# Where 64-bit weights are loaded and converted: w_out's chunks spread over pass 1, w_in's moved into pass 1

## The chip, the cores and the metric

The kernel runs on one core of one Trainium2 chip. The metric is the time of one execution on the device in microseconds (us); runs are summarised by their median.

## What is computed

The reference chains three stages. The first is the real part of a two-dimensional Fourier transform of `x` (8 batches of 3072 rows and 256 columns):

```
X = np.fft.fft(x, axis=1)
X = np.fft.fft(X, axis=2)
return X.real.astype(np.float32)
```

Its 24576 rows then pass through a soft mixture of experts (8 experts with 4 slots each), and last through a layer with a squared ReLU:

```
logits = x @ phi
d = softmax of logits over all rows;  slot_input = d.T @ x
slot_out[e] = np.maximum(slot_input[e] @ w1[e], 0.0) @ w2[e]
c = softmax of logits over slots;     x = c @ slot_out
h = x @ w_in;  r = np.maximum(h, 0.0);  g = s * (r * r) + b
return g @ w_out
```

The weights `w_in` (256 x 2048) and `w_out` (2048 x 256) come as 64-bit floats. There is no 64-bit arithmetic on the chip's engines here, so the kernel loads them as pairs of 32-bit words and puts 32-bit floats together from them.

## The kernel before

The work runs in stages, and x is read twice from memory.

**Pass 1.** x comes in 24 pages of 1 MB (`load_x`, L282), three for each of the 8 batches, numbered here x0 to x23 in the order of loading. Each batch is worked on in two halves n = 2b and 2b + 1, so n runs from 0 to 15. The even half needs the batch's first two pages, the odd half its third. In `emit_v` (L383) TensorE multiplies x with the projected transform matrix into `vt`; ScalarE copies that out (L392); in `turn_v` (L401) TensorE transposes it into `vq`, and either ScalarE or VectorE copies that into `v` (L405), whichever a planner in the code believes to be free. When all four batches of a half are in `v`, `emit_t` (L420) transforms along the rows, one unit of four matmuls into `tps` at a time. There are 16 units. Each is copied into `tt` by eight small copies (L432), all eight on ScalarE for an even unit and on VectorE for an odd one. Eight units are done between n = 8 and n = 15, the other eight after the last half of x. The next stage, the logits (`lp`, L523), reads all of `tt`.

**The logits and pass 2.** After the logits and their maximum, pages of x are loaded a second time in another layout (`load_xr`, `xrt`, L316), again 24, and summed with the softmax weights into `racc` (L679). Then come the experts: `e_up` reads eight pages `w1t` (L851), `e_turn` transposes, and `e_down` reads eight pages `w2t` (L879). The last and longest stage is the layer with w_in and w_out over 64 blocks of rows (L996 to L1035).

**Pages.** Almost all of these tiles come out of one ring of 15 pages, with 5 more from the end of pass 1 on. A transfer into a page waits for the last reader of what stood there. All large transfers are issued by SyncE in the order in which the code asks for them, so one that waits for its page holds up those behind it.

**The 64-bit weights.** Each of the two matrices comes in four chunks of 1 MB (`raw`, issued at L148). For each chunk VectorE runs `double_steps`: shift, two combinations, a mask and a multiplication (L152, L156, L160, L164, L172), then a maximum (L198 for w_out, L216 for w_in). A chunk's raw page is given back after L172. For w_out, GpSimd also adds up the rows for the bias (L267). After w_out's fourth chunk the scale follows: a maximum over the four (L229), a transposition on TensorE (`mx`, L233), two small steps, and then the split of the scaled weights into two 16-bit parts (L259 on VectorE, L261 on ScalarE, L262 on GpSimd). The same three small steps for w_in's maximum (`wim_steps`) come as soon as all of w_in is converted, and at the latest inside `e_down`.

**What sets the order.** In pass 1 the string `ORDER` (L289) gives the order of the transfers: `x` a page of x, `w` a chunk of w_out, `l` and `h` the tables `ltab` and `htab_t`. `pump_a` issues them as far as pages and a lead in estimated time allow. In pass 2 and after, the list `todo` (L762 on) is worked through as pages come free. `side_step` and `fill` put the conversions' steps between the other instructions by estimated times; once built, each engine's order is fixed, and an instruction that waits holds up all that stand behind it on its engine.

Of the kernel before, what the change touches and what calls it, by code (L numbers as in the profile page):

```python
# [32 lines left out]
def tile_fft2__then__softmoe__then__act_relu2(  # L33
# [60 lines left out]
    def page(shape, dt, name, among=9):  # L94
        k = next(k for k, p in enumerate(pools[:among]) if p[2] < p[1])
        pools[k][2] += 1
        return pools[k][0].tile(shape, dt, tag="page", name=name), k

    def free_pages(among=9):
        return sum(max(p[1] - p[2], 0) for p in pools[:among])  # L100
# [4 lines left out]
    todo = []  # L105
    side_work = []
    at = {"pe": 5.0, "act": 0.0, "dve": 0.0, "dma": 3.8}

    def dma_ready(cost=2.93):

        at["dma"] = max(at["dma"], at["pe"] - 1.0) + cost
        return at["dma"] + 1.3
# [10 lines left out]
    side_at, raws, doubles = {}, [0], []  # L123
# [18 lines left out]
    def double_steps(d, src, pool):  # L142

        w = 1024
        raw, rk = page([P, w, 2], U32, "raw")
        raws[0] += 1
        hi, lo = raw[:, :, 1], raw[:, :, 0]
        nc.sync.dma_start(out=raw.rearrange("p w t -> p (w t)"), in_=src.bitcast(U32))  # L148
        f = d.bitcast(U32)

        def s1():
            nc.vector.tensor_scalar(out=f, in0=hi, scalar1=3, scalar2=0x3FFFFFF8,  # L152
                                    op0=ALU.logical_shift_left, op1=ALU.bitwise_and)

        def s2():
            nc.vector.scalar_tensor_tensor(out=f, in0=hi, scalar=0xC0000000, in1=f,  # L156
                                           op0=ALU.bitwise_and, op1=ALU.bitwise_or)

        def s3():
            nc.vector.scalar_tensor_tensor(out=f, in0=lo, scalar=29, in1=f,  # L160
                                           op0=ALU.logical_shift_right, op1=ALU.bitwise_or)

        def s4():
            nc.vector.tensor_scalar(out=hi, in0=hi, scalar1=0x7FF00000, scalar2=None, op0=ALU.bitwise_and)  # L164
            if pool:
                nc.gpsimd.tensor_scalar(out=hi.bitcast(F32), in0=hi, scalar1=float(0x38100000), scalar2=None, op0=ALU.is_ge)
                nc.gpsimd.tensor_tensor(out=d, in0=d, in1=hi.bitcast(F32), op=ALU.mult)
                done()

        def s5():  # L170
            if not pool:
                nc.vector.scalar_tensor_tensor(out=d, in0=hi, scalar=float(0x38100000), in1=d, op0=ALU.is_ge, op1=ALU.mult)  # L172
                done()

        def done():
            drop(rk)
            raws[0] -= 1

        return [(0.0, s1, 0.65), (0.0, s2, 1.15), (0.0, s3, 1.15), (0.0, s4, 0.65), (0.0, s5, 0.0 if pool else 1.15)]
# [28 lines left out]
    def wi_load(k):  # L208
        if k % 2 == 0:
            t, kk = page([P, FF2], F32, "wi", 2)  # L210
            wi.append(t)
            wik.append(kk)
        c, h = divmod(k, 2)
        d = wi[c][:, 1024 * h:1024 * h + 1024]
        steps = double_steps(d, w_in[c * P:(c + 1) * P, 1024 * h:1024 * h + 1024], False)
        steps.append((0.0, lambda: nc.vector.tensor_reduce(  # L216
            out=wim4[:, k:k + 1], in_=d, axis=AX.X, op=ALU.max, apply_absolute_value=True), 1.15))
        side_at[4 + k] = dma_ready()
        side_work.extend((4 + k, *f) for f in steps)
# [59 lines left out]
    def load_x():  # L279
        n = len(xa)  # L280
        t, k = page([P, 2, 8, P], F32, "xb")
        nc.sync.dma_start(out=t, in_=xt[3 * (n // 3) + (0, 2, 1)[n % 3]])  # L282
        xa.append((t, k))
        x_at.append(dma_ready())
# [1 line left out]
    NX = 3 * B  # L286
    CR = 1.5
    LEAD, TOL, LT, LX, HX = 14.0, 0.5, 0, 0, 1
    ORDER = "xxwxwxwxwxxxxxxxxxxxxxxxllhh"  # L289
    tpool = tc.alloc_tile_pool(name="tpool", bufs=1)  # L290
    doubles += [((3, 1, 3, 1)[k], lambda k=k: wo_load(k)) for k in range(4)]

    order = list(ORDER)

    def order_step():
        k = order.pop(0)
        if k == "w":
            doubles.pop(0)[1]()
        elif k == "l":
            ltab_load(len(ltabs))  # L300
        elif k == "h":
            htab_load(len(htabs))
        else:
            load_x()

    def pump_a():

        while order and at["dma"] < at["pe"] + LEAD and free_pages() >= (doubles[0][0] if order[0] == "w" else 1):
            order_step()

    x_at, pend_t, xr = [], [], []
# [24 lines left out]
    def htab_load(i):  # L336

        t, k = page([R, 16, 2, 4 * MH], F32, "htab_t")
        htabs.append((t, k))
        nc.gpsimd.memset(t[32:64], 0.0)  # L340
        for q in range(2):
            nc.sync.dma_start(out=t[64 * q:64 * q + M], in_=htab[:, 32 * i:32 * i + 32].rearrange("r (k q) m -> r k q m", q=2))
        dma_ready(2.5)
# [5 lines left out]
    def ltab_load(i):  # L349
        t, k = page([P, 32, P // 2], F32, "ltab")  # L350
        ltabs.append((t, k))
        for c in range(2):
            nc.sync.dma_start(out=t[NR * c:NR * c + NR], in_=ltab[64 * c:64 * c + M, 32 * i:32 * i + 32].rearrange(
                "(j g) q m -> g j q m", j=2)[0:NR // 2])
        dma_ready(1.2)

    with tc.tile_pool(name="xtp", bufs=1, side="right") as xtp, tc.tile_pool(name="vp", bufs=1, side="right") as vp, \
# [94 lines left out]
        for n in range(NV + 1):  # L452
            if n < NV:
                emit_v(n)
                pump_a()
                fill()
            if n == 3:
                tp = psv.tile([P, P], F32, tag="tps", name="tp", bufs=4)
                nc.tensor.transpose(tp, f_sb, ident)
                nc.vector.tensor_copy(ft_sb, tp)  # L460
            if n >= 1:
                turn_v(n - 1)
            for _ in range(4):
                if pend_t and n < NV:
                    emit_t()
            fill()
            pump_a()
        while order:
            order_step()
# [279 lines left out]
    def w1_load(e):  # L749
        t, wk[0, e] = page([P, 2, FF1], F32, "w1t")  # L750
        nc.sync.dma_start(out=t, in_=w1[e].rearrange("(c p) f -> p c f", p=P))
        w1t[e] = t
        dma_ready()

    def w2_load(e, h=2):
        if h in (0, 2):
            w2t[e], wk[1, e] = page([P, FF1 // P, D], F32, "w2t")
        c = (slice(0, 4), slice(4, 6), slice(0, 8), slice(6, 8))[h]
        dma_ready(2.93 * (0.5, 0.25, 1, 0.25)[h])
        nc.sync.dma_start(out=w2t[e][:, c], in_=w2[e].rearrange("(c p) d -> p c d", p=P)[:, c])  # L760

    todo += [(0, lambda: nc.sync.dma_start(out=dd, in_=dft_d.rearrange("j (c p) d -> p j c d", p=P)))]  # L762
    left = NS1 - len(xr) - sum(t[1] is load_xr for t in todo)
    todo += [(1, load_xr)] * (left - 6)
    for k in range(4):
        todo += [(2 - k % 2, lambda k=k: wi_load(k), 1 - k % 2), (1, load_xr)]
    todo += [(1, load_xr)] * 2
    todo += [(1, lambda e=e: w1_load(e)) for e in range(8)] + [(1, lambda e=e: w2_load(e)) for e in range(4)]
    todo += [(h == 0, lambda e=e, h=h: w2_load(e, h)) for h in (0, 1, 3) for e in range(4, 8)]
    pump()  # L770
# [168 lines left out]
    with tc.tile_pool(name="fr", bufs=4) as frp, tc.tile_pool(name="fo", bufs=3) as fo, \  # L939
# [104 lines left out]
        at = [k * 48 // (16 - 3) for k in range(16 - 3)]  # L1044
# [118 lines left out]
```

## Time and profile before

| | us |
|---|---|
| median of 3 runs | 1433.32 |
| lowest and highest run | 1432.83, 1433.5 |
| the profiled execution, its own time | 1434.0 |
| its span in the trace | 1432.2 |
| TensorE busy in the span | 1384.2 |
| VectorE busy | 1176.8 |
| ScalarE busy | 946.3 |
| GpSimd busy | 323.2 |

The span runs from the first to the last instruction that the profiler recorded, and the rest of the execution's own time lies around it. TensorE is busy for 97% of the span, but its share differs by stage, and a busy TensorE here also counts matmuls that run slowly. What a change in one stage is worth has to be read in that stage.

### The profile page before, as it was taken

Reading aid. Unit: us, or ns where it says so; the run is one execution under the profiler, and the core shown is the slowest. Engines: PE = TensorE matmul, PEld = TensorE weight load, DVE = VectorE, ACT = ScalarE, POOL = GpSimd, SP = SyncE. Lnnn points to the kernel's source line nnn. Section 1 sums busy time; section 2 is a strip of 40 time slices with the busy share of each in tenths; the row PEclk is TensorE's granted clock in tenths of the full one; section 3 lists DMA queues with packets and bytes.
Section 4 is the critical chain, followed back from the end, with each engine's and each line's share of the span. In section 5 each row is a group of like instructions: output and inputs, shape, how many; then the busy total and the mean of one; then the engine's idle time right before and its main releaser. Section 6 shows DMA issues by size and latency. Waiting matters only on the chain.

```text
span 1432.2 us, 23062 instructions
## 1 busy us (share of the span) xinstructions
PE 1384.2 (97%) x8930; PEld 841.2 (59%) x8930; DVE 1176.8 (82%) x1536; ACT 946.3 (66%) x1411; POOL 323.2 (23%) x298
## 2 busy tenths in 40 slices
PE   6796998899999999999999999999999999999998
PEld 4476654556666666666666666666666666666665
DVE  2767753798989898998989888888888888888885
ACT  1255510677777777777777777777777777777773
POOL 1521600431212121222222222121212121111110
PEclk9898999999999999999999999999999999999999
DMA  8995599010101010101010101010101010101000
GB/s 344 416 289 223 210 401 343 16 40 23 36 23 32 23 36 23 35 23 36 23 35 23 36 23 32 23 36 23 36 23 36 22 36 23 36 23 33 23 23 27
DMA packets 81198, 113.41 MB, mean 79 GB/s; under 512 B 35808, under 2 KB 69984, under 8 KB 74304
## 3 DMA queue, kind: packets, MB, share of 16 engines
q1 hardware_dynamic: 80960, 111.83, 23.0%
q8 instruction: 70, 1.15, 0.3%
q14 instruction: 40, 0.33, 0.1%
q0 software_dynamic: 128, 0.10, 0.0%
HBM read 79.00 MB, written 25.17 MB: 73 GB/s over the span
## 4 chain that ended last, share of the span: by engine, by line
PE 89%; DVE 5%; DMA 3%; ACT 1%; SPq 1%; issue 1%; POOL 0%; POOLq 0%; ACTq 0%
PE op L1023 45%; PE op L1025 23%; PE fhp L996 11%; PE racc L679 3%; PE vt L383 2%; DMA raw<-in_moe_w_out_dram 1%; DMA w2t<-in_moe_w_dram 1%; DVE tt L432 1%; PE dps L664 1%; DVE r L1001 1%; PE tps L420 1%; PE lp L523 1%; PE ehp L851 0%; POOL dt L584 0%; PE hp L604 0%
## 5 line engine op out<-in xcount | busy, mean ns | idle before, releaser
L1023 PE MATMUL op<-whl,rhl 128*128 128x512 f16 x3072 | 1025.9, 379 | 0.0
L1025 PE MATMUL op<-whl,rhl 128*128 128x256 f16 x3072 | 837.4, 273 | 0.3 <-DVE rhl L987 0.3
L1000 ACT ACTIVATE r<-fhp 128x768 f32<-128x768 f32 x512 | 413.1, 808 | 192.7 <-PE fhp L996 189.9
L1001 DVE SCALAR_TENSOR_TENSOR r<-fhp,r 128x768 f32<-128x768 f32 x512 | 483.9, 949 | 24.4 <-ACT r L1000 22.8
L1023 PEld LDWEIGHTS <-rhl 128*128 128x128 f16 x3072 | 300.5, 98 | 335.1
L987 DVE TENSOR_TENSOR rhl<-r,rhl 128x768 f16<-128x768 f32 x500 | 489.6, 981 | 3.2 <-ACT rhl L986 0.9
L986 ACT CAST rhl<-r 128x768 f16<-128x768 f32 x508 | 420.1, 827 | 78.1 <-DVE r L1001 77.7
L1033 POOL TENSOR_TENSOR o<-o,bias 128x256 f32<-128x256 f32 x186 | 198.3, 1066 | 886.2 <-ACT o L1032 886.2
L1025 PEld LDWEIGHTS <-rhl 128*128 128x128 f16 x3072 | 300.6, 98 | 62.7 <-DVE rhl L987 0.7
L996 PE MATMUL fhp<-ct,g 128*128 128x384 f16 x1024 | 249.9, 326 | 3.7 <-DVE r L1001 2.9
L1035 DVE SCALAR_TENSOR_TENSOR ot<-op,small,o 128x256 f32<-128x256 f32 x192 | 92.7, 483 | 105.0 <-POOL o L1033 104.8
L996 PEld LDWEIGHTS <-g 128*128 128x128 f16 x1024 | 100.1, 98 | 71.2 <-issue 3.5
L1032 ACT ACTIVATE o<-op,small 128x256 f32<-128x256 f32 x186 | 88.2, 474 | 23.3 <-PE op L1025 22.6
L383 PE MATMUL vt<-xb,phd 128*64 128x512 f32 (+3 forms) x288 | 54.7, 512 | 14.8 <-DMA xb<-in_x_turned_dram 14.8
L392 ACT COPY vts<-vt 128x512 f32<-128x512 f32 (+1 forms) x16 | 8.5, 532 | 60.5 <-PE vt L383 60.4
L383 PEld LDWEIGHTS vt<-xb,phd 128*64 128x64 f32 x288 | 26.5, 149 | 37.2 <-issue 23.5
L679 PE MATMUL racc<-xrt,dh 128*64 128x256 f32 x384 | 44.3, 382 | 0.0
L679 PEld LDWEIGHTS racc<-xrt,dh 128*64 128x64 f32 x384 | 26.4, 137 | 21.0 <-issue 6.0
L987 POOL TENSOR_TENSOR rhl<-r,rhl 128x768 f16<-128x768 f32 x12 | 20.2, 1701 | 60.0 <-DMA g<-gs 53.7
L405 DVE COPY v<-vq 128x512 f32<-128x512 f32 (+1 forms) x11 | 6.6, 598 | 32.2 <-PE vq L401 32.2
L432 DVE COPY tt<-tps 32x256 f32<-32x256 f32 x64 | 26.9, 420 | 1.6 <-PE tps L420 0.8
L432 ACT COPY tt<-tps 32x256 f32<-32x256 f32 x64 | 23.2, 363 | 6.3 <-PE tps L420 5.6
(212 smaller groups left out, 547.3 us busy)
## 6 DMA issues: line engine op xcount, KB each, us to landing
xb<-in_x_turned_dram SPq DMA_DIRECT2D x24, 1024.0 KB, 19.5
xrt<-in_x_pages_dram SPq DMA_DIRECT2D x24, 1024.0 KB, 8.3
out_dram<-ot SPq DMA_DIRECT2D x128, 128.0 KB, 1.7
w1t<-in_moe_w_dram SPq DMA_DIRECT2D x8, 1024.0 KB, 9.7
out_dram<-ot SPq DMA_DIRECT2D x128, 64.0 KB, 2.0
raw<-in_moe_w_out_dram SPq DMA_DIRECT2D x4, 1024.0 KB, 18.2
raw<-in_moe_w_in_dram SPq DMA_DIRECT2D x4, 1024.0 KB, 7.3
w2t<-in_moe_w_dram SPq DMA_DIRECT2D x4, 1024.0 KB, 11.7
```

What stands on the lines that cost most here:

```text
L383: nc.tensor.matmul(vt[64 * h:64 * h + 64, o:o + k, :], lhsT=phd[:, c, sg, :], rhs=turned(pg, c, i, k, rev), start=(c == 0 and m < 2), stop ...
L679: nc.tensor.matmul(raccs[acc][64 * h:64 * h + 64, :], lhsT=dh[:, m, g].rearrange("p j e -> p (j e)"), rhs=xr[k][0][:, g, t, :], start=(sum ...
L986: (nc.vector.tensor_copy if n < 2 and p % 4 == 2 else nc.scalar.copy)(a, r2)
L987: (nc.gpsimd if far else nc.vector).tensor_tensor(out=l, in0=r2, in1=a, op=ALU.subtract)
L996: nc.tensor.matmul(hp[:, k, :].rearrange("p (s b m) -> p s b m", s=2, b=B), lhsT=g16[:, f * P:(f + 1) * P], rhs=c, start=True, stop=True)
L1000: nc.scalar.activation(out=r, in_=hp, func=AF.Relu, scale=1.0 / (CS * CS))
L1001: nc.vector.scalar_tensor_tensor(out=r2, in0=hp, scalar=0.0, in1=r, op0=ALU.max, op1=ALU.mult)
L1023: nc.tensor.matmul(op.rearrange("p h d -> p (h d)"), lhsT=a, rhs=w.rearrange("p h d -> p (h d)"), start=(f == 0), stop=False)
L1025: nc.tensor.matmul(op[:, 0, :], lhsT=l, rhs=w[:, 0, :], start=False, stop=(f == NFC - 1))
L1032: nc.scalar.activation(out=o1, in_=op[:, 1, :], func=AF.Copy, scale=qv)
L1033: nc.gpsimd.tensor_tensor(out=o1, in0=o1, in1=bias, op=ALU.add)
L1035: nc.vector.scalar_tensor_tensor(out=ot, in0=op[:, 0, :], scalar=qv, in1=o1, op0=ALU.mult, op1=ALU.add)
```

## The change

`ORDER` is rewritten: one chunk of w_out now follows the first five pages of x, and then one each three pages; a new letter `W` stands for a chunk of w_in, and four of them stand between pages x15 and x20. The loads of w_in leave the list of pass 2, which now has the second reading of x alone. The steps of the conversion themselves are unchanged. That w_in's two converted pages are now taken in pass 1 leaves two pages fewer for other loads from there on.

```
     LEAD, TOL, LT, LX, HX = 14.0, 0.5, 0, 0, 1
-    ORDER = "xxwxwxwxwxxxxxxxxxxxxxxxllhh"
+    ORDER = "xwxxxwxxxwxxxwxxWxWxxWxWxxxxllhh"
...
+    wi_at = [0]
 
     def order_step():
         k = order.pop(0)
         if k == "w":
             doubles.pop(0)[1]()
+        elif k == "W":
+            wi_load(wi_at[0])
+            wi_at[0] += 1
...
-        while order and at["dma"] < at["pe"] + LEAD and free_pages() >= (doubles[0][0] if order[0] == "w" else 1):
+        while order and at["dma"] < at["pe"] + LEAD and free_pages() >= (doubles[0][0] if order[0] == "w" else 2 - wi_at[0] % 2 if order[0] == "W" else 1):
...
     left = NS1 - len(xr) - sum(t[1] is load_xr for t in todo)
-    todo += [(1, load_xr)] * (left - 6)
-    for k in range(4):
-        todo += [(2 - k % 2, lambda k=k: wi_load(k), 1 - k % 2), (1, load_xr)]
-    todo += [(1, load_xr)] * 2
+    todo += [(1, load_xr)] * left
```

The changed file is longer, so its lines between here and the end of pass 1 are named 5 higher than those of the kernel before. Three places show what moves.

**SyncE's queue in pass 1.** The kernel before issues its transfers in this order, after the three small constants:

```order
L282 DMA xb<-in_x_turned_dram 128x2048 x6
L148 DMA raw<-in_moe_w_out_dram 128x4x512
L282 DMA xb<-in_x_turned_dram 128x2048
L148 DMA raw<-in_moe_w_out_dram 128x4x512
L282 DMA xb<-in_x_turned_dram 128x2048
L148 DMA raw<-in_moe_w_out_dram 128x4x512
L282 DMA xb<-in_x_turned_dram 128x2048
L148 DMA raw<-in_moe_w_out_dram 128x4x512
L282 DMA xb<-in_x_turned_dram 128x2048 x15
L353 DMA ltab<-in_ltab_dram 32x1x2048 x4
```

In the changed kernel, from page x11 on (the first three chunks of w_out stand behind x4, x7 and x10):

```order
L282 DMA xb<-in_x_turned_dram 128x2048 x3
L148 DMA raw<-in_moe_w_out_dram 128x4x512
L282 DMA xb<-in_x_turned_dram 128x2048 x2
L148 DMA raw<-in_moe_w_in_dram 128x2048
L282 DMA xb<-in_x_turned_dram 128x2048
L148 DMA raw<-in_moe_w_in_dram 128x2048
L282 DMA xb<-in_x_turned_dram 128x2048 x2
L148 DMA raw<-in_moe_w_in_dram 128x2048
L282 DMA xb<-in_x_turned_dram 128x2048
L148 DMA raw<-in_moe_w_in_dram 128x2048
L282 DMA xb<-in_x_turned_dram 128x2048 x4
L358 DMA ltab<-in_ltab_dram 32x1x2048 x4
```

w_out's last chunk moved from behind x8 to behind x13, and four more transfers stand ahead of the last pages of x.

**VectorE's queue from w_out's scale to the end of pass 1.** Before (after the scale's small steps; the rows with x40 are one unit and the four of the end):

```order
L259 TENSOR_SCALAR wo<-wo,small 128x512 x8
L405 COPY v_111<-vq 128x32x16
L273 TENSOR_SCALAR bias<-bp,sb_in 128x256
L405 COPY v_111<-vq 128x32x10
L405 COPY v_112<-vq 128x32x16
L432 COPY tt<-tps 32x64x4 x8
...
L405 COPY v_112<-vq 128x32x10
L405 COPY v_112<-vq 128x32x16
L432 COPY tt<-tps 32x64x4 x40
```

In the changed kernel the split stands behind a first unit of copies into `tt` and the scale; `wi` is w_in. Behind the rows shown follow the second and third chunk of w_in with one more unit between their steps, then the fourth chunk and `L437 COPY tt<-tps 32x64x4 x40`:

```order
L437 COPY tt<-tps 32x64x4 x8
L229 TENSOR_REDUCE small<-small 128x1
L234 TENSOR_REDUCE small<-mx 1x1
...
L259 TENSOR_SCALAR wo<-wo,small 128x512 x8
L273 TENSOR_SCALAR bias<-bp,sb_in 128x256
L410 COPY v_112<-vq 128x32x10
L152 TENSOR_SCALAR wi<-raw 128x1024
L156 SCALAR_TENSOR_TENSOR wi<-raw,wi 128x1024
L160 SCALAR_TENSOR_TENSOR wi<-raw,wi 128x1024
L164 TENSOR_SCALAR raw<-raw 128x1024
L172 SCALAR_TENSOR_TENSOR wi<-raw,wi 128x1024
L410 COPY v_112<-vq 128x32x16
L437 COPY tt<-tps 32x64x4 x8
```

All 24 steps of w_in moved from pass 2 to here, and seven of the nine copies of `vq` that stood here moved to ScalarE's queue. On TensorE the transposition `mx` (L233) moved from behind the matmuls of n = 6 to behind those of n = 10.

**SyncE's queue at w2's pages**, with what each transfer waits for (`DMAHW` is an earlier transfer on the same lane, the other names the engine whose last reader must be done). Before:

```order
L760 DMA w2t<-in_moe_w_dram 128x8x256 [waits DMAHW4_49,PE_49]
L760 DMA w2t<-in_moe_w_dram 128x8x256 [waits DMAHW5_49,DVE_49]
L760 DMA w2t<-in_moe_w_dram 128x8x256 [waits DMAHW6_49,PE_49]
L760 DMA w2t<-in_moe_w_dram 128x8x256 [waits DMAHW7_49,PE_49]
L760 DMA w2t<-in_moe_w_dram 128x4x256 [waits DMAHW0_49,PE_49]
L760 DMA w2t<-in_moe_w_dram 128x4x256 [waits DMAHW1_49,PE_49]
L760 DMA w2t<-in_moe_w_dram 128x4x256 [waits DMAHW2_49]
L760 DMA w2t<-in_moe_w_dram 128x4x256 [waits DMAHW3_49,DVE_49]
```

After:

```order
L765 DMA w2t<-in_moe_w_dram 128x8x256 [waits DMAHW4_49,PE_49]
L765 DMA w2t<-in_moe_w_dram 128x8x256 [waits DMAHW5_49,PE_49]
L765 DMA w2t<-in_moe_w_dram 128x8x256 [waits DMAHW6_49,PE_49]
L765 DMA w2t<-in_moe_w_dram 128x8x256 [waits DMAHW7_49,PE_49]
L765 DMA w2t<-in_moe_w_dram 128x4x256 [waits DMAHW0_49,PE_49]
```

The waits for VectorE's conversions are gone. The page of the fourth w2 transfer used to be one that `e_up` reads (`w1t`); it is now one that the last sum of pass 2 (`racc`) reads.

## Rows read from the trace of the kernel before

**Rows 1.** Windows: length, busy of PE, PEld, DVE, ACT, POOL; PEclk, DMA share, GB/s.

```profile
13.00:57.00 44.00, 29.90 (x144) 14.53 (x144) 29.03 (x28) 5.29 (x10) 12.20 (x14) 0.88 1.02 412
57.00:99.00 42.00, 41.01 (x268) 26.19 (x269) 21.58 (x46) 20.95 (x50) 20.76 (x18) 0.96 1.01 328
...
154.00:218.00 64.00, 63.25 (x528) 36.50 (x528) 40.96 (x63) 13.81 (x26) 17.48 (x17) 1.00 0.89 346
...
232.00:251.00 19.00, 13.96 (x133) 5.72 (x131) 3.04 (x9) 0.07 (x1) 0.00 (x0) 0.82 1.12 305
```

**Rows 2.** Chain that ended last, end of pass 1: start us, us, what.

```profile
116.70 5.44 PE lp L523 x73
```

**Rows 3.** Timeline of TensorE, pass 1: start us, us, instructions, [idle before].

```profile
13.18 1.98 PE L383 MATMUL vt<-xb,phd 128*64 128x512 f32 x4 [4.55 <-DMA xb<-in_x_turned_dram]
...
49.76 3.29 PE L383 MATMUL vt<-xb,phd 128*64 128x384 f32 x12 [0.42 <-DMA xb<-in_x_turned_dram]
56.70 0.27 PE L233 MATMUL mx<-ident,small 128*1 128x128 f32 x1 [3.65 <-DVE small L229]
```

**Rows 4.** Timeline of VectorE (DVE), pass 1.

```profile
42.60 1.63 DVE L156 SCALAR_TENSOR_TENSOR wo<-raw,wo 128x1024 uint32<-128x1024 uint32 x1
...
58.40 5.06 DVE L259 TENSOR_SCALAR wo<-wo,small 128x512 f32<-128x512 f32 x8
...
66.94 0.48 DVE L273 TENSOR_SCALAR bias<-bp,sb_in 128x256 f32<-128x256 f32 x1 [2.88 <-PE bp L272]
67.34 0.48 DVE L405 COPY v<-vq 128x320 f32<-128x320 f32 x1
71.97 0.69 DVE L405 COPY v<-vq 128x512 f32<-128x512 f32 x1 [4.14 <-PE vq L401]
...
99.09 17.40 DVE L432 COPY tt<-tps 32x256 f32<-32x256 f32 x40 [0.20 <-PE tps L420]
```

**Rows 5.** VectorE's groups by line in 154 to 231: busy us, mean ns.

```profile
L172 DVE SCALAR_TENSOR_TENSOR wi<-raw,wi 128x1024 f32<-128x1024 uint32 x4 | 4.9, 1228 | 0.1
L160 DVE SCALAR_TENSOR_TENSOR wi<-raw,wi 128x1024 uint32<-128x1024 uint32 x4 | 4.9, 1225 | 0.1
L156 DVE SCALAR_TENSOR_TENSOR wi<-raw,wi 128x1024 uint32<-128x1024 uint32 x4 | 4.9, 1215 | 0.0
L216 DVE TENSOR_REDUCE small<-wi 128x1 f32<-128x1024 f32 x4 | 4.9, 1214 | 0.1
L152 DVE TENSOR_SCALAR wi<-raw 128x1024 uint32<-128x1024 uint32 x4 | 2.8, 689 | 1.3 <-DMA raw<-in_moe_w_in_dram 1.2
L164 DVE TENSOR_SCALAR raw<-raw 128x1024 uint32<-128x1024 uint32 x4 | 2.7, 686 | 0.0
```

**Rows 6.** Timeline of GpSimd (POOL), pass 1.

```profile
40.48 4.34 POOL L267 TENSOR_TENSOR bias<-bias,wo 128x256 f32<-128x256 f32 x4 [4.36 <-DVE wo L172]
...
63.28 6.78 POOL L262 TENSOR_TENSOR whl<-wo,whl 128x512 f16<-128x512 f32 x6 [0.89 <-ACT whl L261]
```

**Rows 7.** Timeline of TensorE, e_down and what follows it.

```profile
232.12 0.63 PE L879 MATMUL eop<-w2t,hT 128*32 128x256 f32 x4
233.97 0.62 PE L879 MATMUL eop<-w2t,hT 128*32 128x256 f32 x2 [1.22 <-DMA w2t<-in_moe_w_dram]
236.96 6.08 PE L879 MATMUL eop<-w2t,hT 128*32 128x256 f32 x58 [2.38 <-DMA w2t<-in_moe_w_dram]
243.96 0.27 PE L233 MATMUL mx<-ident,small 128*1 128x128 f32 x1 [0.91 <-DVE small L229]
244.16 5.48 PE L879 MATMUL eop<-w2t,hT 128*32 128x256 f32 x54
249.84 1.05 PE L879 MATMUL eop<-w2t,hT 128*32 128x256 f32 x10 [0.20 <-DMA w2t<-in_moe_w_dram]
250.82 0.38 PE L238 MATMUL mx<-small,ones 1*128 1x1 f32 x2
251.13 0.71 PE L188 MATMUL warm<-ones 128*128 128x128 f32 x4
```

## The prediction

> **What bounds the kernel now.** I read the busy times by stage first, then the chain that ended last, then the timelines of TensorE and VectorE on both sides of the places that the change touches.
>
> The windows [rows 1] show three different regimes. From 13 to 57 us TensorE works 29.90 of 44 us and the DMA queues are full at 412 GB/s: it waits for x. From 57 to 99 it works 41.01 of 42: it is the bound itself, and VectorE beside it has 42 - 21.58 = 20.4 us of idle time. In pass 2, 154 to 218, TensorE works 63.25 of 64 although VectorE also has 40.96 us to do, 25 of them for w_in. From 232 to 251, e_down, it works only 13.96 of 19.
>
> Pass 1 does not end with TensorE's last matmul on x. VectorE copies units into `tt` from 99.09 on, five in a row for 17.40 us, to 116.49 [rows 4], and the logits start at 116.70 [rows 2]. So whatever delays these five units at the end of VectorE's queue delays everything after.
>
> In e_down TensorE waits for pages of w2, 1.22 + 2.38 + 0.20 us, and for w_in's maximum, 0.91 us [rows 7]. The third of these four, like the first two, names the DMA.
>
> **When the data arrive after the change.** TensorE's first matmul starts when x0 lands, at 13.18, and the matmuls at 49.76 start when x10 lands [rows 3]. Between them lie 14 transfers of 1 MB (ten pages, four chunks of w_out), in the order of issue: (49.76 - 13.18) / 14 = 2.613 us each. This pace holds only while SyncE is not held up by pages. By the waits of the new queue, the transfers from x11 on reuse pages whose readers are done well before their turn; the tightest, x21 to x23, wait for the matmuls of n = 10 and 11, while seven transfers are still under way ahead of them. I therefore take the pace as unbroken. Then transfer i lands at 13.18 + 2.613 i: w_out's last chunk (i = 17) at 57.6, x16 (21) at 68.1, w_in's last chunk (27) at 83.7, x23 (31) at 94.2.
>
> For TensorE itself that is no loss: the last half starts with x23 at 94.2, and its 20 matmul records end before 97, about where they end now. The chunks of w_out, one in four instead of every second transfer, no longer starve it in the middle, but it gets x23 later, so nothing is gained either.
>
> **VectorE's queue in pass 1, the term that decides.** The scale of w_out needs a transposition `mx` that stands on TensorE behind the matmuls of n = 10, and these need x16. Until then VectorE has converted w_out's last chunk (57.6 + 6.3 = 63.9) and copied one unit (3.5 us), and waits. After x16 TensorE needs 12 more records, 3.29 us in the like case of x10 [rows 3], which gives 71.3. From `mx` to the first instruction of the split it was 58.40 - 56.70 = 1.70 us [rows 3, 4]. So the split starts at 73.0 instead of 58.40.
>
> From there VectorE has, without a pause (each input is ready by the times above: w_in's chunks land 20 us ahead of their turn and the units are produced before theirs):
> - the split 5.06, the bias 0.48, two copies of `vq`, 0.48 and 0.69 [rows 4]: 6.7 us;
> - four chunks of w_in at 0.689 + 1.215 + 1.225 + 0.686 + 1.228 + 1.214 = 6.26 us [rows 5]: 25.0 us;
> - two units between them at 17.40 / 5 = 3.48 and the five of the end, 17.40 [rows 4]: 24.4 us;
> - the slower steps beside GpSimd. At 42.60 L156 took 1.63 us while GpSimd added up the bias, 40.48 to 44.82 [rows 4, 6], against 1.215 alone [rows 5], so 0.41 more. GpSimd's part of the split now lies beside the first chunk of w_in, three such steps: 1.2 us. Bounds: none, and three in each chunk, 4.9.
>
> Sum: 73.0 + 6.7 + 25.0 + 24.4 + 1.2 = 130.3, against 116.49: the logits start 13.8 us later. The conversion is thus not hidden, though it would nearly fit: the 20.4 us of idle time in 57 to 99 are used, the seven copies of `vq` that go to ScalarE give back some 4 (0.48 to 0.69 each, [rows 4]), but the first 14.6 us are lost waiting for x16.
>
> On a rule of the skill. "SBUF — State Buffer", section "Who interferes with whom" of the Trainium skill, states that VectorE and GpSimd hold the port pair that they share as an exclusive lock, and that the loser blocks for the whole instruction. An instruction of GpSimd's split takes 6.78 / 6 = 1.13 us [rows 6], so by that rule three steps could lose up to 3.4 us, and the sum would come out 2.2 us later; the row shows 0.41 for one step.
>
> **Pass 2 and the experts.** Removing 25 us from VectorE in pass 2 gives nothing by itself, since TensorE was busy there throughout [rows 1]. What it gives is pages. In the kernel before the fourth page of w2 waits for one that e_up reads, because the raw chunks held pages until VectorE had converted them; now all four first pages of w2 wait only for the sums of pass 2, four transfers of 1 MB (some 10.5 us) asked for before e_up starts. The later pieces, 4 MB, are asked for when e_up gives its pages back, as before, but have the queue to themselves and land within 10.5 us and a little, while the first half of e_down runs. w_in's maximum is ready long before.
>
> So e_down runs through: 4 + 2 + 58 + 54 + 10 = 128 records at 5.48 / 54 = 0.1015 us make 13.0 us from 232.12 on, 245.1, and the next instruction follows there instead of at 251.13 [rows 7]: 5.9 us less. The two small matmuls of w_in's maximum come into pass 2 instead, on a full TensorE: 0.27 [rows 7] and about as much for the second, 0.3, so 0.6. Net 5.3. The bounds: only the three waits for w2, less 0.6, is 3.2; all of it with nothing paid is 5.9.
>
> Nothing else moves. xrt's pages are two fewer, but a page is asked for some 12 pages ahead of its use and pass 2 eats 24 in the 64 us of [rows 1], one in 2.7, so it is there in time. The blocks of the last stage are untouched.
>
> **Sum.** 13.8 - 5.3 = 8.5 us later. The profiled execution took 1434.0 for a span of 1432.2, so it would take 1442.5; the median of the runs is 0.7 lower, 1433.3, which gives **1441.8 us**. From what the runs spread, 0.2% (2.9 us) is about the least that counts as a difference.
>
> **The rivals.**
>
> *The DMA queues are the bound in pass 1.* 32 MB have to come in where 28 did, and in 57 to 99 the rate was 328 GB/s [rows 1], though with tables in small pieces. At that rate the 11.1 us from 57 to x16 become 13.9, and all of VectorE's queue slides by 2.8 us: 1444.6. For it speaks the row; against it the 412 GB/s of the stretch with 1 MB transfers alone. At 412 all the way, x16 comes 1.4 us earlier: 1440.4. "DMA: Bandwidth & Descriptors", section "Specifications" of the Trainium skill, gives about 358 GB/s per core from memory; at that, 2.93 us a page, x16 would come 6.7 us later and the time would be 1448.5, but the measured 412 speaks against it.
>
> *The pages of w2 come no sooner.* If some other transfer on SyncE's queue holds them up, e_down keeps its waits and only the loss stays: 1433.3 + 13.8 + 0.6 = 1447.7. For it: sixteen transfers share eight lanes. Against it: the waits by page that the new queue has.
>
> *VectorE's queue absorbs it (the other side).* If the split could start early, the conversion would fill idle time, pass 1 would end where it does now, and the 5.3 us of e_down would remain: 1428.0. It decides at a gain where the five units end at 121.8, that is with the split at 64.5; x16 would have to land at 59.6, 2.2 us a page or 475 GB/s. No row shows that.
>
> *Gain and loss cancel*, at a point between (split at 64.5): 1433.
>
> **How the numbers follow.** Chances: my forecast 0.70, DMA slower 0.10, w2 no sooner 0.08, absorbed 0.07, cancelled 0.05. The forecast's own range: everything at its low bound (x16 1.4 earlier, no slower steps, 5.9 gained) is 13.8 - 2.6 - 5.9 = 5.3, so 1438.6; the upper bound of the slower steps alone adds 3.7, so 1445.5. To hold 8 in 10 I reach up to the rival of w2 and a little below the low bound: 1437 to 1447.7. Faster by over 0.2%: 0.07; within: 0.06; slower: 0.87.
>
> **What would show it.** Right: VectorE idle shortly before `mx`, then solid from about 73 to 130; the first `lp` matmul at 129 to 132; no wait for w2 in e_down and about 13 us for its 128 records; pass 2's length unchanged within 1 us. Wrong: `lp` before 125 (x came faster, or the split didn't wait for x16), or gaps in VectorE's queue where I have none, waiting for units or chunks; in e_down any wait for w2 over 1 us.

## The result, and the profile after

The changed kernel takes 1445.33 us (median of four runs, 1444.34 to 1445.74); the kernel before took 1433.07 beside it (four runs, 1431.3 to 1433.5). The ratio is 1.0087, 95% interval 1.0069 to 1.0104: 12.3 us slower, where 8.5 were forecast (1441.8, range 1437.0 to 1447.7). The profiled execution took 1444.34 with a span of 1442.6, 10.3 more than the one of before.

Windows of the changed kernel (columns as in [rows 1]); its line numbers are 5 higher in pass 1 and 2 higher from the loop of pass 2 on.

```profile
13.00:57.00 44.00, 36.11 (x190) 18.66 (x186) 20.82 (x22) 7.92 (x16) 7.98 (x11) 0.90 1.02 413
57.00:99.00 42.00, 32.57 (x190) 19.49 (x190) 35.99 (x50) 18.22 (x42) 18.68 (x14) 0.92 1.02 348
99.00:117.00 18.00, 11.88 (x100) 10.46 (x99) 17.58 (x22) 15.57 (x43) 7.14 (x6) 1.00 0.94 304
171.00:235.00 64.00, 63.58 (x531) 36.67 (x530) 22.61 (x47) 13.62 (x25) 17.48 (x17) 1.00 0.92 352
249.00:262.00 13.00, 11.38 (x133) 5.18 (x133) 2.64 (x7) 0.37 (x1) 0.00 (x0) 1.00 1.09 279
```

Against [rows 1] the roles of 57 to 99 are exchanged: TensorE falls from 41.01 to 32.57 us, VectorE (third busy time) rises from 21.58 to 35.99 and stays full after 99. In pass 2 VectorE falls from 40.96 to 22.61, and TensorE is as full as before. The last line is e_down: its granted clock is 1.00 (2.4 GHz throughout), where [rows 1] have 0.82.

Timeline of VectorE, pass 1, to be read beside [rows 4] and [rows 5]:

```profile
70.37 0.28 DVE L234 TENSOR_REDUCE small<-mx 1x1 f32<-1x128 f32 x1 [4.60 <-PE mx L233]
...
71.77 6.88 DVE L259 TENSOR_SCALAR wo<-wo,small 128x512 f32<-128x512 f32 x8
...
79.36 0.86 DVE L152 TENSOR_SCALAR wi<-raw 128x1024 uint32<-128x1024 uint32 x1
80.25 2.06 DVE L156 SCALAR_TENSOR_TENSOR wi<-raw,wi 128x1024 uint32<-128x1024 uint32 x1
82.34 2.06 DVE L160 SCALAR_TENSOR_TENSOR wi<-raw,wi 128x1024 uint32<-128x1024 uint32 x1
84.33 1.65 DVE L164 TENSOR_SCALAR raw<-raw 128x1024 uint32<-128x1024 uint32 x1
...
105.91 2.60 DVE L172 SCALAR_TENSOR_TENSOR wi<-raw,wi 128x1024 f32<-128x1024 uint32 x1
...
116.23 17.38 DVE L437 COPY tt<-tps 32x256 f32<-32x256 f32 x40
```

VectorE waits 4.60 us for `mx`, and then has no idle time over half a microsecond until 133.61. The five last units, which started at 99.09 before, start at 116.23. Timeline of TensorE, where it waits for x, and at the logits and e_down ([rows 2, 3, 7] before):

```profile
65.64 4.49 PE L388 MATMUL vt<-xb,phd 128*64 128x384 f32 x12 [2.53 <-DMA xb<-in_x_turned_dram]
70.06 0.27 PE L233 MATMUL mx<-ident,small 128*1 128x128 f32 x1
...
93.16 4.49 PE L388 MATMUL vt<-xb,phd 128*64 128x384 f32 x12 [2.64 <-DMA xb<-in_x_turned_dram]
...
133.82 1.52 PE L528 MATMUL lp<-tt,ltab 64*64 64x128 f32 x12 [21.58 <-issue]
...
239.95 7.08 PE L853 MATMUL ehp<-w1t,si 128*32 128x512 f32 x64
249.03 4.15 PE L881 MATMUL eop<-w2t,hT 128*32 128x256 f32 x70
254.06 6.18 PE L881 MATMUL eop<-w2t,hT 128*32 128x256 f32 x48 [0.88 <-DMA w2t<-in_moe_w_dram]
260.48 1.05 PE L881 MATMUL eop<-w2t,hT 128*32 128x256 f32 x10 [0.24 <-DMA w2t<-in_moe_w_dram]
261.46 0.71 PE L188 MATMUL warm<-ones 128*128 128x128 f32 x4
```

The ledger: the logits start 17.1 us later (116.70 to 133.82; forecast 13.8). From there to e_down it is 115.2 us instead of 115.4. e_down takes 12.43 instead of 19.01, 6.6 less (forecast, with what moves into pass 2, 5.3). 17.1 - 0.2 - 6.6 = 10.3.

### The profile page after: what moved, and what is told of

Read it like the earlier page. It is cut to its first block, busy times and chain, and to the rows that moved or that the text cites. A ratio compares the mean times of both kernels' runs of the same rounds, so it can differ in the third digit from the quotient of the medians.

```text
span 1442.6 us, 23073 instructions
## 1 busy us (share of the span) xinstructions
PE 1381.3 (96%) x8930; PEld 838.9 (58%) x8930; DVE 1175.8 (82%) x1528; ACT 950.4 (66%) x1419; POOL 323.9 (22%) x298
## 4 chain that ended last, share of the span: by engine, by line
PE 86%; DMA 7%; DVE 3%; issue 1%; ACT 1%; SPq 1%; POOL 0%; POOLq 0%; ACTq 0%
PE op L1025 45%; PE op L1027 23%; PE fhp L998 11%; DMA xb<-in_x_turned_dram 3%; PE racc L684 3%; DMA raw<-in_moe_w_out_dram 3%; DMA w2t<-in_moe_w_dram 1%; PE dps L669 1%; PE vt L388 1%; DVE r L1003 1%; PE hp L609 1%; DVE cm L543 0%; POOL dt L589 0%; PE lp L528 0%; DVE rhl L989 0%
## 5 line engine op out<-in xcount | busy, mean ns | idle before, releaser
L674 DVE COPY dh<-dps 128x512 f32<-128x512 f32 (+1 forms) x14 | 9.1, 651 | 36.6 <-PE dps L669 35.3
L684 PEld LDWEIGHTS racc<-xrt,dh 128*64 128x64 f32 x384 | 26.4, 137 | 21.0 <-issue 6.7
L528 PE MATMUL lp<-tt,ltab 64*64 64x128 f32 (+1 forms) x256 | 12.4, 308 | 23.1 <-issue 21.6
L437 DVE COPY tt<-tps 32x256 f32<-32x256 f32 x64 | 26.9, 420 | 1.0 <-PE tps L425 0.2
## 6 DMA issues: line engine op xcount, KB each, us to landing
w2t<-in_moe_w_dram SPq DMA_DIRECT2D x4, 1024.0 KB, 10.8
```

Of the source, the lines that this page charges most:

```text
L684: nc.tensor.matmul(raccs[acc][64 * h:64 * h + 64, :], lhsT=dh[:, m, g].rearrange("p j e -> p (j e)"), rhs=xr[k][0][:, g, t, :], start=(sum ...
```

## The experiments

The kernel before ran beside all of them, at 1433.6 to 1434.15. One caution on single traces: five kernels below (e1, both e6, e7, e10) have the same pass 1, and their logits start at 109.04, 109.36, 107.92, 113.50 and 108.31. A start of the logits from one trace is thus good to about 3 us; the medians are good to 1 or 2. (109.7, in some expectations, is e1's start read from a row that a window cuts.)

### Which part of the change costs

**e1: w_out's part alone** (on the kernel before).

```diff
-    ORDER = "xxwxwxwxwxxxxxxxxxxxxxxxllhh"
+    ORDER = "xwxxxwxxxwxxxwxxxxxxxxxxllhh"
```

> Only w_out's part of the change: its chunks one in four transfers, w_in's chunks and their conversion in pass 2 as in the kernel before. My theory (the end of pass 1 is the sum of VectorE's queue): the split starts at about 72 instead of 58.4, but VectorE then has only 7 units and two small copies left, and its last five units start at 99 as before, when TensorE has produced them. So the logits start at 116.5 to 118, e_down keeps its waits, and the time is 1433 to 1435. Rival, the late scale and split cost by themselves (VectorE idle before them is simply lost): the logits start up to 13 us later, 1438 to 1446.

Measured: 1425.17, ratio 0.9936 [0.9922, 0.9949], 8.6 us faster than before. Both theories missed. Its windows, VectorE and TensorE:

```profile
13.00:57.00 44.00, 34.17 (x189) 17.38 (x189) 20.15 (x21) 7.42 (x15) 7.98 (x11) 1.00 1.02 413
```

```profile
68.25 4.16 DVE L259 TENSOR_SCALAR wo<-wo,small 128x512 f32<-128x512 f32 x8
...
91.42 17.40 DVE L432 COPY tt<-tps 32x256 f32<-32x256 f32 x40 [0.20 <-PE tps L420]
```

```profile
87.53 2.37 PE L383 MATMUL vt<-xb,phd 128*64 128x384 f32 x20 [0.64 <-DMA xb<-in_x_turned_dram]
...
109.04 2.37 PE L523 MATMUL lp<-tt,ltab 64*64 64x128 f32 x26 [9.39 <-issue]
```

The late split is no loss here: it starts 9.9 us later than before, and the five last units start 7.7 us earlier. From 13 to 57 TensorE runs 189 matmul records instead of 144, at a granted clock of 1.00 instead of 0.88, because pages of x no longer stand behind every second transfer, and it is the bound afterwards; its last half starts at 87.53 instead of 95.19.

**e2: w_in's part alone** (on the changed kernel).

```diff
-    ORDER = "xwxxxwxxxwxxxwxxWxWxxWxWxxxxllhh"
+    ORDER = "xxwxwxwxwxxxxxxxWxWxxWxWxxxxllhh"
```

> Only w_in's part: w_out's chunks loaded as in the kernel before, every second transfer, w_in's chunks between x16 and x20 as in the changed kernel. My theory: the split starts near 58.4, w_in's conversion follows it, and VectorE's queue from there (6.9 split, 1.7 bias and copies, 25 conversion, about 2 beside GpSimd, 24.4 units) ends at 118.4, but its last five units can't start before x23's half, which came 4.5 us later than before in the changed kernel, so 121; logits at 119 to 122, e_down shorter by 6.6 as in the changed kernel: 1430 to 1433. Rival, the 4 MB more through the DMA queues in pass 1 are what costs: the logits as late as in the changed kernel, 1443 to 1446.

Measured: 1440.99, 1.0049 [1.0037, 1.0062]; logits at 129.89, e_down 12.55. My numbers were 8 us too low. VectorE:

```profile
58.24 5.06 DVE L259 TENSOR_SCALAR wo<-wo,small 128x512 f32<-128x512 f32 x8
...
66.74 0.48 DVE L273 TENSOR_SCALAR bias<-bp,sb_in 128x256 f32<-128x256 f32 x1 [2.84 <-PE bp L272]
...
71.77 0.69 DVE L410 COPY v<-vq 128x512 f32<-128x512 f32 x1 [4.14 <-PE vq L406]
...
76.14 0.70 DVE L152 TENSOR_SCALAR wi<-raw 128x1024 uint32<-128x1024 uint32 x1
```

The split is 13.5 us earlier than in the changed kernel, but the logits only 3.9: VectorE now waits 2.84 and 4.14 us for TensorE in the middle, since w_in's first step stands behind a unit in its queue, and starts at 76.14 instead of 79.36.

**e3: w_in's transfers without most of the conversion** (L156, L160, L164 and L172 are left out for w_in, so its sign, exponent and low bits are not put together).

```diff
...
+        if short:
+            return [(0.0, lambda: (s1(), done()), 0.65)]
         return [(0.0, s1, 0.65), (0.0, s2, 1.15), (0.0, s3, 1.15), (0.0, s4, 0.65), (0.0, s5, 0.0 if pool else 1.15)]
```

> The changed kernel with all its transfers, but of w_in's conversion VectorE does only the first step and the maximum (L152, L216), 7.6 us instead of 25 and the slowing; the exponent, sign and low bits of w_in are left out. My theory: VectorE's queue no longer ends last by itself; its five last units start when x23's half has been turned, 103.5, and end at 121; logits at 120 to 122, e_down as in the changed kernel: 1430 to 1433. Rival, DMA is what delays pass 1: logits still at 130 or later, 1440 to 1446.

Measured: 1430.48, 0.9974 [0.9964, 0.9984]; logits at 119.86. As my theory had it: VectorE now waits for x23's half before its last units. TensorE and then VectorE:

```profile
95.60 4.53 PE L390 MATMUL vt<-xb,phd 128*64 128x384 f32 x20 [3.09 <-DMA xb<-in_x_turned_dram]
```

```profile
101.22 0.69 DVE L412 COPY v<-vq 128x512 f32<-128x512 f32 x1 [6.39 <-PE vq L408]
102.24 17.40 DVE L439 COPY tt<-tps 32x256 f32<-32x256 f32 x40 [0.33 <-PE tps L427]
```

The last units start 10.8 us later than in e1. Of these, 8.1 are the later landing of x23 (95.60 against 87.53), and 2.2 the 20 records on it, which took 4.53 us at a granted clock of 0.50 (96 to 100) after a wait of 3.09, and 2.37 in e1. The transfers are thus a bound of their own, at 119.9, under the one that VectorE sets at 133.8.

**e4: without GpSimd's part of the split** (w_out's low halves are left out: zero).

```diff
             whl.append(page([P, 8, 2, D], F16, "whl")[0])
+            nc.gpsimd.memset(whl[-1][:, :, 1, :], 0.0)
...
-        nc.gpsimd.tensor_tensor(out=whl[h][:, k, 1, :], in0=wo[h][:, k], in1=whl[h][:, k, 0, :], op=ALU.subtract)
```

> The changed kernel without GpSimd's part of the split (the low halves of w_out are zero, set when the page is loaded, so they are left out of the result). My theory: the split takes 5.1 instead of 6.9 us and the first w_in chunk's steps that lay beside it lose their slowing, L156 and L160 1.22 instead of 2.06 us: logits 3.2 to 4.6 us earlier, 129.2 to 130.6, time 1440.7 to 1442.1. Rival, the steps are slow for another reason (the clock, or ScalarE's copies reading the same tiles): split and chunk as slow as in the changed kernel, 1445.

Measured: 1438.21, 1.0032 [1.0022, 1.0042], 7 us less than the changed kernel; logits at 128.00, 5.8 earlier:

```profile
72.18 3.26 DVE L260 TENSOR_SCALAR wo<-wo,small 128x512 f32<-128x512 f32 x8
...
76.87 1.23 DVE L156 SCALAR_TENSOR_TENSOR wi<-raw,wi 128x1024 uint32<-128x1024 uint32 x1
...
110.42 17.38 DVE L437 COPY tt<-tps 32x256 f32<-32x256 f32 x40
```

The split starts 0.4 later than in the changed kernel and the last units 5.8 earlier. The gain is more than I expected, because the split alone takes 3.26 us, not 5.06: the row of before was itself slowed.

**e5: two of VectorE's five last units on ScalarE** (on the changed kernel).

```diff
-        eng = "act" if q % 2 == 0 else "dve"
+        eng = "act" if q % 2 == 0 or (bg == 1 and q in (3, 7)) else "dve"
```

> The changed kernel with two of VectorE's five last units (16 copies of 32x256) on ScalarE, which had finished its own four at 117.35 while VectorE worked to 133.6. My theory (VectorE's queue is what ends pass 1): VectorE ends 7 us earlier, ScalarE with six units at about 123.4, logits at 126.8, time 1438.3 (1437 to 1440). Rival, the transfers end pass 1 (x23's half): logits still at 133 or no more than 2 us earlier, 1443.5 to 1445.5.

Measured: 1438.77, 1.0037 [1.0024, 1.0051]: 6.6 us less than the changed kernel; logits at 128.48. ScalarE ends its six units at 118.96, and VectorE's three end last:

```profile
117.82 10.41 DVE L437 COPY tt<-tps 32x256 f32<-32x256 f32 x24
```

So VectorE's queue, and not x, ends pass 1 of the changed kernel.

### What shortens e_down

**e6: w_in asked for earlier in pass 2** (on e1; after 4 pages of xrt instead of 8, and in a second version, with 12 and 8 in place of 10 and 6, after 2).

```diff
-    todo += [(1, load_xr)] * (left - 6)
+    todo += [(1, load_xr)] * (left - 10)
...
-    todo += [(1, load_xr)] * 2
+    todo += [(1, load_xr)] * 6
```

> The kernel with w_out's chunks spread and w_in in pass 2, but w_in's four chunks are asked for after 4 pages of xrt instead of 8, so their raw pages are free earlier. My theory (what shortens e_down in the changed kernel is only that the raw chunks give their pages back before w2 asks for them): the logits stay at 109.7, pass 2 keeps its length within 1 us, and of e_down's wait for w2 (1.31 + 2.39 + 0.21) and for w_in's maximum most is gone: 3 to 6.5 us less than with the spread alone, 1419 to 1422. Rival, the wait in e_down is not due to these pages but to the transfers themselves, or TensorE then waits for xrt in pass 2: 1425 or later.

> As the run before, with w_in's chunks asked for after only 2 pages of xrt. My theory: pages free earlier still, all of e_down's waits gone as far as in the changed kernel (6.6 us shorter), 1418.5 to 1421, unless xrt's pages come late in pass 2, which would show as TensorE waiting for xrt. Rival as there: 1425 or later.

Measured: 1427.26 (0.9960 [0.9945, 0.9974]) and 1425.89 (0.9944 [0.9932, 0.9957]): nothing gained over e1. In the second, e_down waits for w2 as ever and takes 19.56 us:

```profile
223.46 1.01 PE L879 MATMUL eop<-w2t,hT 128*32 128x256 f32 x4
226.85 0.62 PE L879 MATMUL eop<-w2t,hT 128*32 128x256 f32 x2 [2.38 <-DMA w2t<-in_moe_w_dram]
229.87 5.97 PE L879 MATMUL eop<-w2t,hT 128*32 128x256 f32 x58 [2.39 <-DMA w2t<-in_moe_w_dram]
```

From this I took it, wrongly, that megabytes and not pages are what counts.

**e7: a quarter of w_in's bytes** (on e1; the other three quarters are copies).

```diff
...
-        steps = double_steps(d, w_in[c * P:(c + 1) * P, 1024 * h:1024 * h + 1024], False)
+        steps = double_steps(d[:, 0:256], w_in[c * P:(c + 1) * P, 1024 * h:1024 * h + 256], False, 256)
+        steps.append((0.0, lambda: nc.vector.tensor_copy(d.rearrange("p (r w) -> p r w", w=256)[:, 1:4], d[:, 0:256].unsqueeze(1).to_broadcast([P, 3, 256])), 0.65))
```

> The kernel with w_out's chunks spread and w_in in pass 2 as before, but of each chunk of w_in only a quarter is loaded (256 of 1024 columns) and copied to the other three, so three quarters of w_in are left out: the transfers, the raw pages and the order stay, with 3 MB less for the DMA queues in pass 2. Old theory (pages): w2's fourth page still waits for one that e_up reads, so e_down keeps its waits, 1425. New theory (from the runs with w_in early, where that wait was gone and e_down no shorter: the DMA queues are full from some 50 us after the logits start until e_down ends, so what counts is how many MB they still have to move then, 35.0 in the runs with w_in in pass 2 and 32.2 in the changed kernel): e_down's waits go by 4 to 6.6 us as in the changed kernel, 1418.5 to 1421.5.

Measured: 1424.24, 0.9939 [0.9925, 0.9952]; e_down 16.84. 3 MB less gave 1.3 us of e_down against e1's 18.13, and nothing that the medians can tell from e1.

**e10: both at once** (e7's edit, and `left - 14`).

> Both at once: w_in asked for ahead of the last 14 pages of xrt, so that no first page of w2 waits for one that e_up reads, and only a quarter of each chunk loaded (three quarters of w_in are copies, so left out). The two runs before showed each alone to give nothing: early pages alone left 9.6 MB to move after e_up begins, fewer MB alone 8.4, the changed kernel 6.8. New theory (e_down ends when w2's last pages have landed, so it needs both the pages early and 3 MB less in the queue): at e_up's start no more than 6.8 MB are left, e_down takes 12.4 to 13.5 us instead of 18.1, time 1418.5 to 1421. Rival: e_down's wait is due to something else in pass 2 that only the changed kernel removes: 1424 to 1426.

Measured: 1424.92, 0.9937 [0.9923, 0.9950]; e_down 18.76, with waits of 1.90 and 2.39. So bytes alone are not the reason either. The trace shows what I had overlooked in e6 as well: a raw chunk gives its page back at VectorE's pace, not when it was asked for. Where VectorE reads the last one,

```profile
205.64 0.43 DVE L171 SCALAR_TENSOR_TENSOR wi<-raw,wi 128x256 f32<-128x256 uint32 x1
```

it is 205.64, in e6's second version 206.00, in e1 218.12. That is 12 us earlier than in e1, and still too late: the first three chunks are read out here at 162.92, 178.94 and 195.73, so two of the four still hold their pages when SyncE asks for w1's first page at 188.63. In e6's second version it is two as well, in e1 three.

**e11: the pages alone** (on the changed kernel, with neither transfer nor conversion; a condition is changed too, so that w_in's maximum need not wait for the small copies).

```diff
+    def hold(k):
+        t, r = page([P, 2], F32, "hold")
...
+        def step(m):
+            nc.vector.tensor_copy(t[:, 1:2], t[:, 0:1])
+            if m == 4:
+                drop(r)
...
-    todo += [(1, load_xr)] * left
+    todo += [(1, load_xr)] * (left - 6)
+    for k in range(4):
+        todo += [(1, lambda k=k: hold(k)), (1, load_xr)]
+    todo += [(1, load_xr)] * 2
```

> The changed kernel, and in pass 2 four idle pages in the places that w_in's raw chunks had in the kernel before: each is taken in the queue where a chunk was, touched by six tiny copies on VectorE where the conversion's steps were, and given back with the fifth. No transfer and no conversion is added, the result is the same. The run with early pages and a quarter of the bytes kept its waits, so bytes in the queue can't be the whole reason. Theory (pages): holding these pages alone makes the pages of w1 and w2 come later, and e_down takes 16 to 18 us again instead of 12.4, waits for w2 of over 2 us: 1448.5 to 1451. Rival (bytes): e_down stays at 12.4 to 13.5 us, 1444 to 1446.5.

Measured: 1454.44, 1.0137 [1.0120, 1.0154], 9 us over the changed kernel. Part of that is pass 1, whose logits start at 136.38 in this trace; e_down takes 19.58:

```profile
251.79 1.00 PE L896 MATMUL eop<-w2t,hT 128*32 128x256 f32 x4
255.18 0.62 PE L896 MATMUL eop<-w2t,hT 128*32 128x256 f32 x2 [2.39 <-DMA w2t<-in_moe_w_dram]
258.20 6.15 PE L896 MATMUL eop<-w2t,hT 128*32 128x256 f32 x64 [2.40 <-DMA w2t<-in_moe_w_dram]
```

Held pages alone bring the waits back. The mark of it is when SyncE asks for the first page of w1. In the kernel before, and then in the changed one:

```profile
197.49 17.81 SPq L751 DMA_DIRECT2D w1t<-in_moe_w_dram  x8
```

```profile
209.00 18.99 SPq L756 DMA_DIRECT2D w1t<-in_moe_w_dram  x8
```

In the changed kernel and in e2 to e5 that is 30.9 us before e_up (209.00 for 239.95), and e_down takes 11.8 to 12.6 us; in the kernel before, e1, e6, e7 and e10 it is 25.5, in e9 26.4, here 22.2, and e_down takes 16.8 to 19.8. From that first request to e_down's last ten matmul records, which wait for w2's last page, it is 50.1 to 54.0 us in all thirteen traces. e_down thus ends when the pages of w1 and w2 are in, and what the changed kernel does is to ask for them sooner. Bytes have a small part in it: in e7, with 3 MB less ahead of it, w1's first page lands 6.2 us after its request, in e1 9.4.

### A version that beats both

**e9: w_out spread, w_in loaded behind the tables, converted in pass 2.**

```diff
-    ORDER = "xwxxxwxxxwxxxwxxWxWxxWxWxxxxllhh"
+    ORDER = "xwxxxwxxxwxxxwxxxxxxxxxxllhhWWWW"
...
-        for _ in range(4):
-            load_xr()
```

> w_out's chunks spread as in the changed kernel, w_in's four chunks asked for behind x23 and behind the tables, in place of the first pages of xrt, and converted in pass 2, where TensorE is the bound. My theory: x and the tables come as with the spread alone, VectorE's queue in pass 1 has no conversion, so the logits start at 109.7; the pages of xrt asked for early are 8 instead of 12 while 4 MB of w_in are in, so some 32.5 MB instead of 35.0 remain for the stretch in which the DMA queues are full, and e_down is 3 to 6 us shorter: 1419 to 1422.5. Rival, what delays pass 1 in the changed kernel is any 4 MB more before the logits: logits at 119, 1430 to 1435. Other rival: xrt's pages come late in pass 2 because the raw pages hold theirs, TensorE waits there, 1425 or later.

Measured: 1426.04, 0.9951 [0.9938, 0.9965]; logits at 106.67, but e_down 19.75, for the same reason as in e6: all four raw chunks were asked for by 90, but VectorE reads them out only at 163.79, 177.49, 189.55 and 203.41, and w1 is asked for from 187.50 on, when two of them still hold their pages. It beats both kernels by what e1 does, and e1, which is simpler, beats both as well (1425.17).

## Why the prediction was right, and where it was not

The direction, the range and both large terms held. Point by point:

- **"The term that decides" is VectorE's queue in pass 1: right in kind.** e5 moves two units off VectorE's queue and gets 6.6 us back; e3 takes most of the conversion away and gets 14.8. The term was 13.8 and measured 17.1, so the first `lp` matmul, at 133.82, came just outside the 129 to 132 that I had named as a sign.
- **The slower steps beside GpSimd were mis-sized, and that is more than the whole 3.3.** The queue is 61.8 us long (71.77 to 133.61) where I had 57.3: the split with what follows it 1.5 longer, the first chunk 2.7, the third 1.35, the fourth 0.3; 5.8 in place of my 1.2, above even my bound of 4.9. Against it stands the split 1.2 us earlier than forecast: x16 came at 65.64 (2.53 us a transfer instead of 2.613), but the 12 records after it took 4.49 us instead of 3.29. e4 shows the cause of the first two: the split with what follows it took 8.2 us and the first chunk 8.9, and without GpSimd's subtraction 4.6 and 6.1. The third chunk's 1.35 lies beside GpSimd's copy of a table (L172, 2.60). My error was to price from one row, 1.63 beside the bias sum, and to take 5.06 for the split's own time: alone it is 3.26 (e4), so 1.8 of the slowing were in that row already. The rule of the Trainium skill that I had set aside ("SBUF — State Buffer", section "Who interferes with whom": the shared ports are locked for a whole instruction) was the nearer one: its sum, 2.2 us later, would have been 132.5.
- **"The first 14.6 us are lost waiting for x16": in the main not the cause.** In e1 the split stands behind x16's matmuls as well, 9.9 us later than before, and e1 is 8.6 us faster; in e2 it starts 13.5 us earlier than in the changed kernel, and only 3.9 of them come back at the logits, because VectorE's waiting moves behind it. What costs most in the changed kernel is the conversion itself (14.0, below). Whether another order of VectorE's queue could hide it in pass 1 was not tried.
- **"Nothing is gained either" by spreading w_out: wrong.** By itself that part of the change is a gain of 8.6 us. It cannot be seen in the changed kernel, because w_in's four transfers take it back. By one trace each, so to about 3 us, the 17.1 us are: spread -7.7 (e1), w_in's transfers +10.8 (e3 against e1), the rest of its conversion, with the slowing, +14.0 (the changed kernel against e3).
- **e_down: right in mechanism, 1.3 short in size.** It is the pages, as forecast (e11 shows it). But I had put it on one page, w2's fourth; in e6's second version that one no longer waits for e_up, but the third does (3.0 us), and nothing is gained. All pages of w1 and w2 come earlier in the changed kernel. And "e_down runs through" was wrong twice over, with errors that cancel, so that my 13.0 us came near the measured 12.43 by luck. Waits for w2 are left (0.88 and 0.24): the last pages land while the second half of e_down runs and not the first, the very last at 260.4. And my 0.1015 us is not the price of a record: the 54 records that it came from [rows 7] ran at a granted clock of 1.00 (244.1 to 249.7), and waits of TensorE's weight loads for w2 are in it, shown below. The changed kernel's first 70 took 4.15, 0.059 each, the next 48, with such waits, 0.129. (251.13 less 245.1 is also 6.0 and not 5.9.)
- **Pass 2's length** from its first transposition (`htp`) to e_up, 69.1 instead of 68.8 with w_in's maximum in it: right.
- **The rivals.** "Absorbed" was not near: even with most of the conversion left out the logits start at 119.9 (e3). "DMA is the bound" is the next bound underneath, but not the one that decided (e5). x23 came at 99.47, 5.3 us after its forecast; in 84 to 99 the rate was 222 GB/s, with the tables' small pieces asked for at 80. Whether these held x23 up was not tried, and in the changed kernel it cost nothing, since VectorE was busy to 116.

The weight loads (PEld) of e_down, before and then after:

```profile
246.85 0.57 PEld L879 LDWEIGHTS eop<-w2t,hT 128*32 128x32 f32 x10 [0.61 <-DMA w2t<-in_moe_w_dram]
```

```profile
257.42 0.57 PEld L881 LDWEIGHTS eop<-w2t,hT 128*32 128x32 f32 x10 [0.62 <-DMA w2t<-in_moe_w_dram]
```

Between the 10.3 us of the two traces and the 12.3 of the medians lie 2 us: the profiled run of the changed kernel is the lowest of its four, 1.0 under their median, and that of the kernel before, 1434.0, lies 0.9 above the median beside it.

## What to carry to other kernels

Split a change that bundles two moves before you believe its sum: here one half was worth 8.6 us, and the other hid it. Work that is moved into another engine's idle time must be placed against when that idle time falls, what stands ahead of it in the queue, and who shares its ports then. When a transfer is late, ask how long each buffer of its ring is held, and by which engine's pace; asking for data earlier frees its page only as early as its reader is done with it.

## What the runs showed of the hardware

A two-input instruction of VectorE (L156, L160: 1.22 us alone) took 2.06 beside GpSimd's subtraction. L172 (1.23 alone) started at 105.91 and took 2.60 beside GpSimd's table copy, which ran from 105.55 to 107.44: about the time to the copy's end and then its own. GpSimd in pass 1 of the changed kernel:

```profile
72.99 12.44 POOL L262 TENSOR_TENSOR whl<-wo,whl 128x512 f16<-128x512 f32 x8 [8.99 <-PE tps L425]
...
105.55 1.89 POOL L481 COPY ltab<-ltab 64x2048 f32<-64x2048 f32 x1 [0.90 <-DMA ltab<-in_ltab_dram]
```

Beside a memset, which only writes, the two-input L160 lost nothing, while the one-input L164 (0.69 alone) doubled. From e2, VectorE and then GpSimd:

```profile
84.38 1.22 DVE L160 SCALAR_TENSOR_TENSOR wi<-raw,wi 128x1024 uint32<-128x1024 uint32 x1
...
89.08 1.43 DVE L164 TENSOR_SCALAR raw<-raw 128x1024 uint32<-128x1024 uint32 x1
```

```profile
84.20 1.48 POOL L345 MEMSET htab_t<- 32x1664 f32 x1 [14.30 <-PE vt L388]
88.47 1.48 POOL L345 MEMSET htab_t<- 32x1664 f32 x1 [2.79 <-PE vt L388]
```

The Trainium skill, "SBUF — State Buffer", section "Who interferes with whom", says so: with two inputs in SBUF VectorE contends with GpSimd's reads and not with its writes alone, and `tensor_scalar` in its two-port mode contends with GpSimd altogether. The trace agrees. The maximum (L216) took 1.21 to 1.22 in every place.

TensorE's 12 records after a wait of 2.53 us for x took 4.49 us in the changed kernel (at 65.64, above); the granted clock from 65.6 to 70.1 was 0.62 on average, between its two levels of 1.2 and 2.4 GHz. In e1, after a shorter wait and at 1.00, they took 2.80:

```profile
43.52 2.80 PE L383 MATMUL vt<-xb,phd 128*64 128x384 f32 x12 [0.97 <-DMA xb<-in_x_turned_dram]
```

Here the longer wait for data cost some 1.7 us more than its own length.
